# The hand-over from an expert's output to the next attention: an earlier second score, and small gate products among the long ones

## The chip, the cores and the metric

The kernel runs on one core of a Trainium2 chip. The metric is the device time of one execution in microseconds (us). TensorE multiplies matrices, ScalarE (ACT) and VectorE (DVE) read its results in PSUM, GpSimd (POOL) adds in SBUF, and SyncE (SP) mostly issues transfers.

## The reference

Eight sequences of 384 tokens go through grouped attention (16 heads of q, 4 of k and v, head size 64), and each token's attention output then goes to one of 16 experts, chosen by two softmaxes.

```python
def _attn_ref(q, k, v):
    ...                                      # k and v repeated for their group of 4 heads
    scores = scale * np.matmul(q, k.transpose(0, 1, 3, 2))
    scores = scores - np.max(scores, axis=-1, keepdims=True)
    attn = np.exp(scores)
    attn = attn / (np.sum(attn, axis=-1, keepdims=True) + 1e-09)
    return np.matmul(attn, v)

def _moe_ref(x, w_group, w_expert, w1, w2):  # x: 3072 tokens x 1024
    g_logits = x @ w_group                   # 4 groups
    g_idx = np.argmax(g_logits, axis=1)      # g_w: softmax weight of the chosen group
    for g in range(G):
        ...
        e_logits = xg @ w_expert[g]          # 4 experts a group; e_w likewise
        e_idx = np.argmax(e_logits, axis=1)
        for e in range(Eg):
            ...
            h = np.maximum(xg[mask_e] @ w1[g, e], 0.0)
            ye = h @ w2[g, e]
            out[tok_idx] = combined[:, None] * ye     # combined = g_w * e_w
```

## The kernel before

One sequence is one block `b` of work. The attention of `b` runs in 24 units (4 heads of k and v, 6 slices each). TensorE writes a score, ScalarE takes its exponential into SBUF, and TensorE multiplies that with v two units later.

```python
def score(self, u):
    ...
    sT = ps_tile("s")                        # two such tiles, in turn
    for r in range(2):
        for s in range(2):
            nc.tensor.matmul(out=sT[r * H2:(r + 1) * H2, s, :S], lhsT=kT..., rhs=qT...)   # 64x64
    e = epool.tile([P, 2, S], F32, name="e")
    nc.scalar.activation(e..., sT..., ACT.Exp, scale=scale)                               # line 311
...
def run(self, u0, u1, inserts, nxt=None):
    for u in range(u0, u1):
        if u + 2 < NU:
            self.score(u + 2)                # line 305
        ...
        self.pv(u)                           # line 324: 8 products of e with v
        self.tail(u)                         # adds on GpSimd, reductions on VectorE
        for f in inserts.get(u, []):
            f()
```

Before attention `b` is done, the expert of sequence `b` is not known. The kernel guesses it from the mean of v, works with that expert for the whole sequence, and tokens of other experts are done in a loop at the end. The guess needs 12 products with one column each (the means) and 4 products with 20 columns (the logits of the guess).

```python
def guess_mean(b, pt, eng=None):
    pm = pt[:, 1, :Hkv]
    v16 = vraw[b].rearrange("p h x -> p (h x)").bitcast(BF16)
    for g in range(Hkv):
        for i in range(SC):
            e0 = g * NC * D + i * P
            nc.tensor.matmul(out=pm[:, g:g + 1], lhsT=v16[:, 2 * e0 + 1:2 * (e0 + P):2],  # line 457
                             rhs=onesb[:, :1], start=(i == 0), stop=(i == SC - 1))
    vm = gpool.tile([P, Hkv], BF16, name="vm")
    evac(eng or nc.vector, vm, pm)
    return vm

def guess_logits(vm, glp):
    for g in range(Hkv):
        nc.tensor.matmul(out=glp[:, SC, :], lhsT=vm[:, g:g + 1].to_broadcast([P, P]),     # line 473
                         rhs=wgd[:, g, :], start=(g == 0), stop=(g == Hkv - 1))
```

Between two attentions the expert of the sequence before (`f = b - 1`) is worked off. Its output has three chunks `c` of 128 tokens; each chunk has two halves `nh` of 512 columns, and each half is a sum over 8 products.

```python
def ffn_y(w2, hT, c, which, nhs=(0, 1), y=None):
    if y is None:
        y = ps_tile(which)
    for nh in nhs:
        for f in range(FQ):                  # FQ = 8; line 615
            nc.tensor.matmul(out=y[:, nh, :], lhsT=hT[:, f, c * P:(c + 1) * P],
                             rhs=w2[:, f, nh * HALF:(nh + 1) * HALF],
                             start=(f == 0), stop=(f == FQ - 1))
    return y

def y_out(f, c, y, split=False):
    ...                                      # ScalarE and VectorE copy y times weight; then out
    if split:
        nc.scalar.mul(ot[:, :HALF], y[:, 0, :], weff[b][:, c:c + 1])                      # line 630
        nc.vector.tensor_scalar(ot[:, HALF:], y[:, 1, :], ...)                            # line 631

def block(b):
    last = b == B - 1
    f = b - 1
    ...                                      # transfers, first layer of f (L606), sums, normalise
    moe_y(f, 0, "s")
    cast(b, 2)
    cast(b, 3)
    nc.sync.dma_start(out=xb_dram[b], in_=xb[b])
    y = ffn_y(w2s[f], hTs[f], 1, "s", (0,))
    gate_logits(b, ps_tile("o"))             # line 443: 16 products
    ffn_y(w2s[f], hTs[f], 1, "s", (1,), y)
    y_out(f, 1, y)
    pt = ps_tile("s")
    glp = gate_rows(pt)
    gate_tokens(b, glp)                      # line 468: token logits, 3 products
    vm = None if last else guess_mean(b + 1, pt)
    y = ffn_y(w2s[f], hTs[f], 2, "o", (0,))
    if not last:
        guess_logits(vm, glp)
        at[b + 1] = Attn(b + 1)
        at[b + 1].score(0)
    weights[b] = gate_softmax(b, glp, not last)      # VectorE
    if not last:
        pick_index(b + 1)                            # VectorE
    ffn_y(w2s[f], hTs[f], 2, "o", (1,), y)
    if not last:
        at[b + 1].score(1)
        return {1: [do(y_out, f, 2, y, True)]}       # inserted behind unit 1 of the next attention
    ...
```

`block(b)` is called for b = 2 to 7. The hand-over from block 1 to attention 2 (`first_block`) is built alike, but does its gate work elsewhere.

Of the kernel before, what the change touches and what calls it, by code (L numbers as in the profile page):

```python
# [18 lines left out]
def kernel(  # L19
# [11 lines left out]
    nc = tc.nc  # L31
    P = 128
    B, Hq, S, D = q.shape
    _, Hkv, _, _ = k.shape
    SC = S // P
# [6 lines left out]
    FQ = F // P  # L42
    NW = G + NE
    HALF = DM // 2
# [26 lines left out]
    def ps_tile(which, shape=None, dtype=F32):  # L71
        if which == "x":
            which = f"o{1 - turn['o']}"
        else:
            turn[which] = 1 - turn[which]
            which += str(turn[which])
        return psum.tile(shape or [P, 2, 512], dtype, name="ps_" + which)
# [70 lines left out]
    onesb = cpool.tile([P, 4 * P], BF16)  # L148
# [38 lines left out]
    wgd = cpool.tile([P, Hkv, NW], BF16)  # L187
# [50 lines left out]
    def evac(eng, out_, in_):  # L238
        if eng is nc.scalar:
            eng.copy(out=out_, in_=in_)  # L240
        else:
            eng.tensor_copy(out=out_, in_=in_)  # L242
# [187 lines left out]
    def cast(b, m):  # L430
        ks = slice(2 * m, 2 * m + 2)
        nc.scalar.copy(out=xb[b][:, ks, :], in_=xT[b][:, ks, :])  # L432

    lgs = {}

    def gate_logits(b, pt):
        lg = pt[:, 0]
        for jj in range(KQ // 4):  # L440
            for t in range(4):
                kq = 4 * jj + t
                nc.tensor.matmul(out=lg[32 * t:32 * t + 32, :S], lhsT=wg[:, kq, :],  # L443
                                 rhs=xT[b][:, kq, :],
                                 start=(jj == 0), stop=(jj == KQ // 4 - 1))
        ls = gpool.tile([P, S], F32, name="lgs")
        nc.scalar.copy(out=ls, in_=lg[:, :S])
        lgs[b] = ls

    def guess_mean(b, pt, eng=None):  # L450

        pm = pt[:, 1, :Hkv]
        v16 = vraw[b].rearrange("p h x -> p (h x)").bitcast(BF16)
        for g in range(Hkv):
            for i in range(SC):
                e0 = g * NC * D + i * P
                nc.tensor.matmul(out=pm[:, g:g + 1], lhsT=v16[:, 2 * e0 + 1:2 * (e0 + P):2],  # L457
                                 rhs=onesb[:, :1], start=(i == 0), stop=(i == SC - 1))
        vm = gpool.tile([P, Hkv], BF16, name="vm")
        evac(eng or nc.vector, vm, pm)  # L460
        return vm

    def gate_rows(pt):
        return pt[:, 1, 64:64 + (SC + 1) * NW].rearrange("p (c n) -> p c n", n=NW)

    def gate_tokens(b, glp):
        for c in range(SC):
            nc.tensor.matmul(out=glp[:, c, :], lhsT=lgs[b][:, c * P:(c + 1) * P],  # L468
                             rhs=mod32[:, 0, :NW], start=True, stop=True)

    def guess_logits(vm, glp):
        for g in range(Hkv):
            nc.tensor.matmul(out=glp[:, SC, :], lhsT=vm[:, g:g + 1].to_broadcast([P, P]),
                             rhs=wgd[:, g, :], start=(g == 0), stop=(g == Hkv - 1))

    def gate_softmax(b, glp, guess, eng=None):

# [75 lines left out]
    ers, w1s, w2s = {}, {}, {}  # L553
# [3 lines left out]
    def pick_index(b):  # L557
        oh = oh_first if b == 0 else oh_all[:, b - 1, SC, :]
        key = gpool.tile([P, NE], F32, name="key")
        nc.vector.scalar_tensor_tensor(key, oh, float(NE), eback, op0=ALU.mult, op1=ALU.add)  # L560
        km = gpool.tile([P, 1], F32, name="km")
        nc.vector.tensor_reduce(out=km, in_=key, axis=AX.X, op=ALU.max)
        oh1 = oh1_all[:, b, :]
        nc.vector.tensor_scalar(oh1, key, km, None, op0=ALU.is_ge)
        t1 = gpool.tile([P, NE], F32, name="t1")
        ef = gpool.tile([P, 1], F32, name="ef")
        nc.vector.scalar_tensor_tensor(t1, eidx, 1.0, oh1, op0=ALU.mult, op1=ALU.mult,
                                       accum_out=ef)
        e_i = gpool.tile([P, 1], I32, name="e_i")
        nc.vector.tensor_copy(out=e_i, in_=ef)  # L570
        e_is[b] = e_i
# [35 lines left out]
                                 rhs=x[:, kq, :], start=(kq == 0), stop=(kq == KQ - 1))  # L607
        nc.scalar.activation(hT[:, f0:f0 + 2, :], h[:, :, :S], ACT.Relu)  # L608

    def ffn_y(w2, hT, c, which, nhs=(0, 1), y=None):  # L610
        if y is None:
            y = ps_tile(which)
        for nh in nhs:
            for f in range(FQ):
                nc.tensor.matmul(out=y[:, nh, :], lhsT=hT[:, f, c * P:(c + 1) * P],  # L615
                                 rhs=w2[:, f, nh * HALF:(nh + 1) * HALF],
                                 start=(f == 0), stop=(f == FQ - 1))
        return y

    hTs = {}  # L620

    def moe_h(b, f0, which):
        if f0 == 0:
            hTs[b] = xpool.tile([P, FQ, S], BF16, name="hT", bufs=1)
        ffn_h(xb[b], w1s[b], hTs[b], f0, which)
# [15 lines left out]
    def do(f, *a):  # L641
        return lambda: f(*a)
# [6 lines left out]
    at = {0: Attn(0), 1: Attn(1)}  # L649
    at[0].start()  # L650
    fill(4)
    state, weights = {}, {}
# [11 lines left out]

    def first_guess():
        state["pt"] = ps_tile("x")
        state["vm"] = guess_mean(0, state["pt"], nc.scalar)

    def first_pick():
        glp = gate_rows(state["pt"])  # L670
        guess_logits(state["vm"], glp)
        first_choice(glp)
        pick_index(0)

# [19 lines left out]
    a = at[0]  # L694
# [19 lines left out]
    a = at[1]  # L714
# [10 lines left out]
    pt = ps_tile("x")  # L725
    gate_logits(0, pt)
    moe_h(0, 2, "s")
    glp = gate_rows(pt)
    gate_tokens(0, glp)
    vm = guess_mean(1, pt, nc.scalar)  # L730
    collect(1, 0, 2)
    sums(1, 0, 2, "s")
    for m in range(2):
        normalise(1, m)
    moe_h(0, 4, "s")
    guess_logits(vm, glp)
    weights[0] = gate_softmax(0, glp, True, nc.scalar)
    pick_index(1)
    moe_h(0, 6, "s")
# [3 lines left out]
    def first_block():  # L743

        prefetch(1)
        collect(1, 2, Hkv)
        weights[0]()
        out_weights(0)
        cast(1, 0)
        cast(1, 1)  # L750
        moe_y(0, 0, "s")
        y = ffn_y(w2s[0], hTs[0], 1, "s", (0,))
        sums(1, 2, Hkv, "o")
        normalise(1, 2)
        normalise(1, 3)
        ffn_y(w2s[0], hTs[0], 1, "s", (1,), y)
        y_out(0, 1, y)
        cast(1, 2)
        cast(1, 3)
        nc.sync.dma_start(out=xb_dram[1], in_=xb[1])  # L760
        y = ffn_y(w2s[0], hTs[0], 2, "o", (0,))
        at[2] = Attn(2)
        at[2].score(0)
        ffn_y(w2s[0], hTs[0], 2, "o", (1,), y)
        at[2].score(1)
        return {1: [do(y_out, 0, 2, y, True)], 3: [second_logits], 19: [second_gate],
                21: [second_pick]}

# [3 lines left out]
    def second_gate():  # L772
        state["pt"] = ps_tile("x")
        gate_tokens(1, gate_rows(state["pt"]))
        state["vm"] = guess_mean(2, state["pt"])

    def second_pick():
        glp = gate_rows(state["pt"])
        guess_logits(state["vm"], glp)
        weights[1] = gate_softmax(1, glp, True, nc.scalar)  # L780
        pick_index(2)

# [9 lines left out]
# [3 lines that stand above are left out]
        prefetch(b)  # L795
        moe_h(f, 0, "s")
        collect(b, 0, Hkv)
        weights[f]()
        out_weights(f)
        moe_h(f, 2, "s")  # L800
        sums(b, 0, Hkv, "o")
        for m in range(4):
            normalise(b, m)
        moe_h(f, 4, "s")
        moe_h(f, 6, "s")
        cast(b, 0)
        cast(b, 1)
        moe_y(f, 0, "s")
        cast(b, 2)
        cast(b, 3)  # L810
        nc.sync.dma_start(out=xb_dram[b], in_=xb[b])
        y = ffn_y(w2s[f], hTs[f], 1, "s", (0,))
        gate_logits(b, ps_tile("o"))
        ffn_y(w2s[f], hTs[f], 1, "s", (1,), y)
        y_out(f, 1, y)
        pt = ps_tile("s")
        glp = gate_rows(pt)
        gate_tokens(b, glp)
        vm = None if last else guess_mean(b + 1, pt)
        y = ffn_y(w2s[f], hTs[f], 2, "o", (0,))  # L820
        if not last:
            guess_logits(vm, glp)
            at[b + 1] = Attn(b + 1)
            at[b + 1].score(0)
        weights[b] = gate_softmax(b, glp, not last)
        if not last:
            pick_index(b + 1)
        ffn_y(w2s[f], hTs[f], 2, "o", (1,), y)
        if not last:
            at[b + 1].score(1)  # L830
            return {1: [do(y_out, f, 2, y, True)]}
        y_out(f, 2, y, True)
        weights[b]()
        out_weights(b)
# [26 lines left out]
    for c in range(SC):  # L861
        ot = opool.tile([P, DM], F32, name="ot")
        for nh in range(2):
            y = ps_tile("so"[nh])
# [12 lines left out]
            for i, (ps, x) in enumerate(halves(c)):  # L877
                eng = nc.scalar if (c, nh, i) == (SC - 1, 1, 1) else nc.sync
# [5 lines left out]
    with tc.For_i(0, n_left, 1):  # L884
# [17 lines left out]
        w1, w2 = fetch1(er), fetch2(er)  # L902
# [8 lines left out]
        hT = xpool.tile([P, FQ, S], BF16, name="hT", bufs=1)  # L911
# [4 lines left out]
        for c in range(SC):  # L916
# [3 lines left out]
            y = ffn_y(w2, hT, c, "s")  # L920
# [34 lines left out]
```

The softmax here doesn't subtract the row's maximum and nothing guards it: scores larger than these inputs give would overflow.

## Time and profile before

| | |
|---|---|
| device time, median of 3 runs | 382.23 us (382.09 to 382.82) |
| span of the profiled execution | 380.1 us |
| matmuls on TensorE | 3663 |
| granted TensorE clock, mean | 0.996 |
| VectorE / ScalarE / GpSimd busy | 69% / 61% / 39% of the span |
| moved by DMA | 76.02 MB, 200 GB/s in the mean |

The profile is that of one execution. Its lines name the engine, the line of the kernel, the output and the inputs of a group of instructions, and the shapes. PE is TensorE's multiplying part, PEld its loading of weights, which can overlap. The chain that ended last follows the work back from the last instruction to what released each step, so a step on it is one that the end of the kernel hung on, and "issue" is time in which the engine waited for nothing that the profile shows. The end of a matmul is modelled, while starts are recorded; distances are therefore best taken from start to start.

### The profile page before, as it was taken

The numbers are of one execution on the slowest core, as the hardware profiler recorded it, in microseconds if no ns is written. First come the engines' busy times: TensorE is split into PE (matmuls) and PEld (weight loads), VectorE is DVE, ScalarE is ACT, GpSimd is POOL, SyncE is SP. The second block draws the span as 40 slices with busy tenths as digits, with TensorE's granted clock in tenths as the row PEclk, the third lists the DMA queues.
The fourth block names the chain that finished last, engine by engine and source line by source line (L and its number), as shares of the span: only waits on it lengthen the run. The fifth ranks groups of instructions, "written<-read, shape, count | busy, mean of one in ns | idle before, by whom it ended". The sixth has DMA issues, their size and how long they took to land.

```text
span 380.1 us, 8950 instructions
## 1 busy us (share of the span) xinstructions
PE 364.6 (96%) x3663; PEld 193.9 (51%) x3663; DVE 261.9 (69%) x494; ACT 232.6 (61%) x315; POOL 147.3 (39%) x116
## 2 busy tenths in 40 slices
PE   8999799999989999999999999999999999999992
PEld 3444356444545455545555455554555456554541
DVE  4789978847689279854998279883798449983130
ACT  4779945768824498256953489344982569544321
POOL 5657730716613077212653047330772036600000
PEclk9999999999999999999999999999999999999998
DMA  8975999999999999899999999999998999199734
GB/s 190 247 115 93 238 211 149 241 237 260 207 160 223 252 248 184 173 211 297 213 148 221 228 278 208 148 220 254 244 185 163 182 282 228 30 207 220 236 68 100
DMA packets 71209, 76.02 MB, mean 200 GB/s; under 512 B 35928, under 2 KB 50264, under 8 KB 71168
## 3 DMA queue, kind: packets, MB, share of 16 engines
q0 software_dynamic: 26640, 41.03, 61.8%
q1 hardware_dynamic: 44096, 33.81, 36.1%
q10 hardware_dynamic: 432, 0.61, 0.5%
q8 instruction: 29, 0.48, 0.5%
q14 instruction: 12, 0.10, 0.1%
HBM read 89.21 MB, written 18.87 MB: 284 GB/s over the span
## 4 chain that ended last, share of the span: by engine, by line
PE 78%; DVE 13%; ACT 6%; issue 2%; ACTq 0%; DVEq 0%; POOLq 0%
PE ps_o L324 22%; PE ps_s L606 18%; PE ps_s L615 14%; PE ps_o L615 7%; PE ps_s L305 7%; ACT e L311 4%; DVE red L338 4%; PE ps_o L443 3%; DVE xT L425 2%; DVE rb L416 2%; PE ps_o L268 1%; PE ps_o L606 1%; DVE w L425 1%; PE ps_s L468 1%; PE ps_o L405 1%
## 5 line engine op out<-in xcount | busy, mean ns | idle before, releaser
L331 POOL TENSOR_TENSOR e<-e 128x768 f32<-128x768 f32 x64 | 116.1, 1830 | 138.5 <-ACT e L311 91.5
L311 ACT ACTIVATE e<-ps_s 128x768 f32<-128x768 f32 x192 | 149.1, 819 | 25.2 <-PE ps_s L305 23.5
L324 PE MATMUL ps_o<-e,v_raw 64*64 64x384 f32 x1536 | 153.8, 482 | 1.6 <-DVE xT L425 1.6
L338 DVE TRANSPOSE_TENSOR_REDUCE red<-e 128x24 f32<-128x768 f32 x128 | 114.1, 946 | 10.5 <-POOL e L331 10.5
L606 PE MATMUL ps_s<-xb,w 128*128 128x384 bf16 x480 | 81.0, 326 | 0.0
L324 PEld LDWEIGHTS ps_o<-e,v_raw 64*64 64x64 f32 x1536 | 61.0, 133 | 28.5 <-issue 20.0
L305 PE MATMUL ps_s<-qT,kT 64*64 64x384 bf16 x768 | 67.1, 327 | 3.0 <-ACT e L311 1.7
L608 ACT ACTIVATE hT<-ps_s 128x768 bf16<-128x768 f32 x30 | 24.3, 811 | 70.9 <-PE ps_s L606 70.9
L606 PEld LDWEIGHTS <-w 128*128 128x128 bf16 x512 | 48.8, 98 | 36.3 <-issue 4.8
L615 PEld LDWEIGHTS <-hT 128*128 128x128 bf16 x384 | 36.0, 98 | 45.4 <-issue 5.4
L615 PE MATMUL ps_s<-w,hT 128*128 128x512 bf16 x248 | 56.4, 379 | 0.0
L305 PEld LDWEIGHTS <-kT 64*64 64x64 bf16 x768 | 29.4, 104 | 42.6 <-issue 39.1
L615 PE MATMUL ps_o<-w,hT 128*128 128x512 bf16 x136 | 32.0, 379 | 0.0
L416 DVE STREAM_TRANSPOSE rb<-inv 128x384 f32<-128x384 f32 x60 | 31.1, 557 | 1.0
L425 DVE TENSOR_TENSOR xT<-xT,rb 128x768 f32<-128x768 f32 x26 | 28.2, 1086 | 0.9
L634 ACT ACTIVATE ot<-ps_s,we 128x1024 f32<-128x1024 f32 x14 | 15.6, 1116 | 19.1 <-PE ps_s L615 19.1
L432 ACT CAST xb<-xT 128x768 bf16<-128x768 f32 x28 | 22.1, 832 | 0.0
L371 DVE COPY xT<-ps_o 128x768 f32<-128x768 f32 x22 | 20.2, 919 | 0.0
L242 DVE CAST vm<-ps_s 128x4 bf16<-128x4 f32 x5 | 0.8, 163 | 27.4 <-PE ps_s L457 27.4
L663 POOL COPY after<-qT 128x1 bf16<-128x1 bf16 x7 | 1.3, 189 | 40.5 <-DMA qT<-q_raw 37.5
L631 DVE TENSOR_SCALAR ot<-ps_o,we 128x512 f32<-128x512 f32 x7 | 5.3, 750 | 15.6 <-ACT ot L630 11.3
L409 DVE RECIPROCAL inv<-ps_o 128x96 f32<-128x96 f32 (+2 forms) x10 | 6.0, 603 | 7.0 <-PE ps_o L405 7.0
(129 smaller groups left out, 189.3 us busy)
## 6 DMA issues: line engine op xcount, KB each, us to landing
w<-in_moe_w_dram POOLq DMA_DIRECT2D x16, 2048.0 KB, 21.9
out_dram<-ot SPq DMA_DIRECT2D x42, 256.0 KB, 7.0
xb_scratch<-xb SPq DMA_DIRECT2D x8, 768.0 KB, 9.8
q_raw<-in_q_dram POOLq DMA_DIRECT2D x7, 768.0 KB, 33.6
v_raw<-in_v_dram SPq DMA_DIRECT2D x14, 384.0 KB, 7.3
out_dram<-ot SPq DMA_DIRECT2D x11, 128.0 KB, 2.3
k<-in_k_dram POOLq DMA_DIRECT2D x7, 192.0 KB, 30.3
w<-in_q_dram POOLq DMA_DIRECT2D x3, 192.0 KB, 7.3
```

The lines of the kernel that those rows point to most:

```text
L305: nc.tensor.matmul(out=sT[r * H2:(r + 1) * H2, s, :S], lhsT=kT[b][s * D:(s + 1) * D, slot, ks], rhs=qT[b][s * D:(s + 1) * D, kq * SC:(kq + ...
L311: nc.scalar.activation(e.rearrange("p t (s x) -> p s t x", s=2), sT[:, :, :S].rearrange("p s (t x) -> p s t x", t=2), ACT.Exp, scale=scale)
L324: nc.tensor.matmul(out=oT[t * D:(t + 1) * D, r, :S], lhsT=vraw[b][r * H2:(r + 1) * H2, g, c * D:(c + 1) * D], rhs=self.e[u][r * H2:(r + 1) ...
L331: eng.tensor_add(out=self.e[u], in0=self.e[u], in1=self.e[u + 1])
L338: nc.vector.tensor_reduce(out=reds[self.b][:, g, n].rearrange("p t j -> p (t j)"), in_=self.e[u].rearrange("p t (j x) -> p (t j) x", x=32) ...
L371: nc.vector.tensor_copy(out=dst, in_=src)
L416: nc.vector.transpose(out=rb[:, r].rearrange("p (j x) -> p j x", x=32), in_=inv[b][:, 2 * m + r].unsqueeze(2).to_broadcast([P, NB, 32]))
L425: eng.tensor_mul(out=x, in0=x, in1=rb)
L432: nc.scalar.copy(out=xb[b][:, ks, :], in_=xT[b][:, ks, :])
L606: nc.tensor.matmul(out=h[:, jj, :S], lhsT=w1[:, kq, (f0 + jj) * P:(f0 + jj + 1) * P], rhs=x[:, kq, :], start=(kq == 0), stop=(kq == KQ - 1))
L608: nc.scalar.activation(hT[:, f0:f0 + 2, :], h[:, :, :S], ACT.Relu)
L615: nc.tensor.matmul(out=y[:, nh, :], lhsT=hT[:, f, c * P:(c + 1) * P], rhs=w2[:, f, nh * HALF:(nh + 1) * HALF], start=(f == 0), stop=(f == ...
```

## The change

The second score of the next attention came behind the whole second half of the expert's last chunk. It now comes after three of the eight products of that half, so that ScalarE can begin its exponential while TensorE still has five products to do. `first_block` gets this too. And in blocks 2 to 6 the 12 mean products and the 4 guess products no longer stand in rows of their own: a helper, `weave`, puts them between the products of the middle chunk, the means into its first half and the guess into its second. The means move into the free bank of the tile of the gate logits, the softmax of the gate and the choice of the expert are issued before the first score, and no product is added or left out.

```diff
+    def weave(main, side):
+        k = 0
+        for i, f in enumerate(main):
+            f()
+            while k < len(side) and k * len(main) < (i + 1) * len(side):
+                side[k]()
+                k += 1
 ...
-    def ffn_y(w2, hT, c, which, nhs=(0, 1), y=None):
+    def ffn_y(w2, hT, c, which, nhs=(0, 1), y=None, fs=None, side=()):
         if y is None:
             y = ps_tile(which)
-        for nh in nhs:
-            for f in range(FQ):
-                nc.tensor.matmul(...)
+        weave([mm(...) for nh in nhs for f in (range(FQ) if fs is None else fs)], side)
         return y
+
+    def y_scores(f, a, y):
+        ffn_y(w2s[f], hTs[f], 2, "o", (1,), y, range(FQ // 2 - 1))
+        a.score(1)
+        ffn_y(w2s[f], hTs[f], 2, "o", (1,), y, range(FQ // 2 - 1, FQ))
 ...  # first_block
-        ffn_y(w2s[0], hTs[0], 2, "o", (1,), y)
-        at[2].score(1)
+        y_scores(0, at[2], y)
 ...  # block
-        y = ffn_y(w2s[f], hTs[f], 1, "s", (0,))
-        gate_logits(b, ps_tile("o"))
-        ffn_y(w2s[f], hTs[f], 1, "s", (1,), y)
+        gt = ps_tile("o")
+        y = ffn_y(w2s[f], hTs[f], 1, "s", (0,), side=[] if last else guess_mean(b + 1, gt))
+        gate_logits(b, gt)
+        glp = gate_rows(ps_tile("s"))
+        guess = [] if last else guess_logits(mean_copy(gt, nc.vector), glp)
+        ffn_y(w2s[f], hTs[f], 1, "s", (1,), y, side=guess)
         y_out(f, 1, y)
-        pt = ps_tile("s")
-        glp = gate_rows(pt)
         gate_tokens(b, glp)
-        vm = None if last else guess_mean(b + 1, pt)
         y = ffn_y(w2s[f], hTs[f], 2, "o", (0,))
-        if not last:
-            guess_logits(vm, glp)
-            at[b + 1] = Attn(b + 1)
-            at[b + 1].score(0)
         weights[b] = gate_softmax(b, glp, not last)
         if not last:
             pick_index(b + 1)
+            at[b + 1] = Attn(b + 1)
+            at[b + 1].score(0)
+            y_scores(f, at[b + 1], y)
+            return {1: [do(y_out, f, 2, y, True)]}
         ffn_y(w2s[f], hTs[f], 2, "o", (1,), y)
-        if not last:
-            at[b + 1].score(1)
-            return {1: [do(y_out, f, 2, y, True)]}
```

More of the change, by code (lines that the diff above doesn't have):

```diff
@@ L432, in cast, with mm @@
         nc.scalar.copy(out=xb[b][:, ks, :], in_=xT[b][:, ks, :])
+    def weave(main, side):
[5 more added lines that the diff above has]
+                k += 1
+    def mm(*a, **kw):
+        return lambda: nc.tensor.matmul(*a, **kw)
     lgs = {}
@@ L448, in gate_logits, with guess_mean @@
         lgs[b] = ls
-    def guess_mean(b, pt, eng=None):
+    def guess_mean(b, pt):
         pm = pt[:, 1, :Hkv]
         v16 = vraw[b].rearrange("p h x -> p (h x)").bitcast(BF16)
+        side = []
         for g in range(Hkv):
@@ L456, in guess_mean, with mean_copy, all_of @@
                 e0 = g * NC * D + i * P
-                nc.tensor.matmul(out=pm[:, g:g + 1], lhsT=v16[:, 2 * e0 + 1:2 * (e0 + P):2],
-                                 rhs=onesb[:, :1], start=(i == 0), stop=(i == SC - 1))
+                side.append(mm(out=pm[:, g:g + 1], lhsT=v16[:, 2 * e0 + 1:2 * (e0 + P):2],
+                               rhs=onesb[:, :1], start=(i == 0), stop=(i == SC - 1)))
+        return side
+    def mean_copy(pt, eng):
         vm = gpool.tile([P, Hkv], BF16, name="vm")
-        evac(eng or nc.vector, vm, pm)
+        evac(eng, vm, pt[:, 1, :Hkv])
         return vm
+    def all_of(side):
+        for f in side:
+            f()
     def gate_rows(pt):
@@ L471, in guess_logits @@
     def guess_logits(vm, glp):
-        for g in range(Hkv):
-            nc.tensor.matmul(out=glp[:, SC, :], lhsT=vm[:, g:g + 1].to_broadcast([P, P]),
-                             rhs=wgd[:, g, :], start=(g == 0), stop=(g == Hkv - 1))
+        return [mm(out=glp[:, SC, :], lhsT=vm[:, g:g + 1].to_broadcast([P, P]), rhs=wgd[:, g, :],
+                   start=(g == 0), stop=(g == Hkv - 1)) for g in range(Hkv)]
     def gate_softmax(b, glp, guess, eng=None):
@@ L608, in ffn_h @@
         nc.scalar.activation(hT[:, f0:f0 + 2, :], h[:, :, :S], ACT.Relu)
-    def ffn_y(w2, hT, c, which, nhs=(0, 1), y=None):
+    def ffn_y(w2, hT, c, which, nhs=(0, 1), y=None, fs=None, side=()):
         if y is None:
             y = ps_tile(which)
-        for nh in nhs:
-            for f in range(FQ):
-                nc.tensor.matmul(out=y[:, nh, :], lhsT=hT[:, f, c * P:(c + 1) * P],
-                                 rhs=w2[:, f, nh * HALF:(nh + 1) * HALF],
-                                 start=(f == 0), stop=(f == FQ - 1))
-        return y
+        weave([mm(out=y[:, nh, :], lhsT=hT[:, f, c * P:(c + 1) * P],
+                  rhs=w2[:, f, nh * HALF:(nh + 1) * HALF], start=(f == 0), stop=(f == FQ - 1))
+               for nh in nhs for f in (range(FQ) if fs is None else fs)], side)
+        return y
+    def y_scores(f, a, y):
+        ffn_y(w2s[f], hTs[f], 2, "o", (1,), y, range(FQ // 2 - 1))
+        a.score(1)
+        ffn_y(w2s[f], hTs[f], 2, "o", (1,), y, range(FQ // 2 - 1, FQ))
     hTs = {}
@@ L666, in first_guess @@
         state["pt"] = ps_tile("x")
-        state["vm"] = guess_mean(0, state["pt"], nc.scalar)
+        all_of(guess_mean(0, state["pt"]))
+        state["vm"] = mean_copy(state["pt"], nc.scalar)
     def first_pick():
         glp = gate_rows(state["pt"])
-        guess_logits(state["vm"], glp)
+        all_of(guess_logits(state["vm"], glp))
         first_choice(glp)
@@ L729 @@
     gate_tokens(0, glp)
-    vm = guess_mean(1, pt, nc.scalar)
+    all_of(guess_mean(1, pt))
+    vm = mean_copy(pt, nc.scalar)
     collect(1, 0, 2)
@@ L735 @@
     moe_h(0, 4, "s")
-    guess_logits(vm, glp)
+    all_of(guess_logits(vm, glp))
     weights[0] = gate_softmax(0, glp, True, nc.scalar)
@@ L774, in second_gate @@
         gate_tokens(1, gate_rows(state["pt"]))
-        state["vm"] = guess_mean(2, state["pt"])
+        all_of(guess_mean(2, state["pt"]))
+        state["vm"] = mean_copy(state["pt"], nc.vector)
     def second_pick():
         glp = gate_rows(state["pt"])
-        guess_logits(state["vm"], glp)
+        all_of(guess_logits(state["vm"], glp))
         weights[1] = gate_softmax(1, glp, True, nc.scalar)
@@ L811, in block @@
         nc.sync.dma_start(out=xb_dram[b], in_=xb[b])
-        y = ffn_y(w2s[f], hTs[f], 1, "s", (0,))
-        gate_logits(b, ps_tile("o"))
-        ffn_y(w2s[f], hTs[f], 1, "s", (1,), y)
+        gt = ps_tile("o")
[4 more added lines that the diff above has]
+        ffn_y(w2s[f], hTs[f], 1, "s", (1,), y, side=guess)
         y_out(f, 1, y)
-        pt = ps_tile("s")
-        glp = gate_rows(pt)
         gate_tokens(b, glp)
-        vm = None if last else guess_mean(b + 1, pt)
         y = ffn_y(w2s[f], hTs[f], 2, "o", (0,))
-        if not last:
-            guess_logits(vm, glp)
-            at[b + 1] = Attn(b + 1)
-            at[b + 1].score(0)
         weights[b] = gate_softmax(b, glp, not last)
```

## The prediction

> **What bounds the kernel now.** I read the busy shares first. TensorE is busy for nearly all of the span, and its clock is granted in full (the row of granted clock is nines until the end), so time is lost or won on TensorE's own queue.
>
> ```profile
> PE 364.6 (96%) x3663; PEld 193.9 (51%) x3663; DVE 261.9 (69%) x494; ACT 232.6 (61%) x315; POOL 147.3 (39%) x116
> ```
>
> Next I read the chain that ended last, cut to the place the change touches: the end of the expert's output in the middle of the run and the first units of the attention behind it (columns: start in us, length in us, what).
>
> ```profile
> 168.21 1.43 PE ps_o L443 x16
> 169.63 1.83 PE ps_s L615 x8
> 171.47 0.58 PE ps_s L468 x6
> 172.04 0.28 PE ps_s L457 x12
> 172.33 1.75 PE ps_o L615 x8
> 174.08 0.09 PE ps_s L473 x4
> 174.16 0.29 PE ps_s L305 x4
> 174.45 1.83 PE ps_o L615 x8
> 176.28 0.32 PE ps_s L305 x4
> ...
> 178.08 0.82 ACT e L311
> 178.90 0.58 ACT ot L630
> 179.47 0.71 ACT e L311
> 180.18 0.04 issue
> 180.22 0.36 PE ps_s L305 x4
> 180.58 0.64 PE ps_o L324 x8
> 181.23 0.16 PE ps_s L305 x4
> ```
>
> L443 are gate logits, L468 token logits, L457 the 12 products of the means of v, L473 the four guess products, L615 half a chunk of expert output (8 products), L305 a score, L324 a unit of attention times v. The reader is to see three things. The 12 means take 0.28 us, 23 ns each; the guess products 0.09 us. A score inside the attention takes 0.16 us, but one between two expert halves 0.29, and the half behind it 1.83 instead of 1.75. And from 176.6 to 180.2 the chain runs through ScalarE: the exponentials, with the copy of the expert's output (L630) between two of them.
>
> Windows of a fraction of a microsecond in the timeline give the starts that I calculate with. For TensorE:
>
> ```profile
> 174.09 0.36 PE L305 MATMUL ps_s<-qT,kT 64*64 64x384 bf16 x4
> 174.38 0.39 PE L615 MATMUL ps_o<-w,hT 128*128 128x512 bf16 x1
> ...
> 176.21 0.52 PE L305 MATMUL ps_s<-qT,kT 64*64 64x384 bf16 x8
> ```
>
> and for ScalarE, in windows of its own:
>
> ```profile
> 176.68 0.81 ACT L311 ACTIVATE e<-ps_s 128x768 f32<-128x768 f32 x1 [1.31 <-PE ps_s L305]
> ...
> 178.77 0.70 ACT L630 ACTIVATE ot<-ps_o,we 128x512 f32<-128x512 f32 x1
> 179.34 0.83 ACT L311 ACTIVATE e<-ps_s 128x768 f32<-128x768 f32 x1
> ```
>
> The stretch repeats every 44.2 us: L606's second half starts at 157.72, 201.92, 246.12 and 290.31 in the chain.
>
> **What the Trainium skill says.** "TensorE: Matmul & The Clock Gate", section "Wait — 56ns, not 53.3ns?", has the distance between starts of small matmuls never below about 25 ns, however small they are; the trace's 0.28/12 = 23 ns agrees, and here each also brings its own weights. The same page, section "Step-by-step: what each phase is for", has weight loads pulled ahead of running matmuls into a background buffer; agreed, the 98 ns loads of L615 lie hidden under products that follow each other every 216 ns. "TensorEngine Tiling (Array Packing)", section "Key Properties", says that a change of tiling mode drains TensorE. Agreed: a score (64x64) between expert products (128x128) costs more than one in the stream. "PSUM — Partial Sum Buffer", section "PSUM bank collisions raise a hardware error", asks for guards by bank. The means go to one bank of the tile and gate logits to the other, so VectorE may copy the means while gate logits run; no run shows this yet.
>
> **Part 1, the weave.** It removes no product. It moves 12 means from behind the token logits between the first eight products of chunk 1, and 4 guess products between its second eight. Could weight loads now vanish under the long products? A mean's load does. But the next long product's load can then start only once the mean has taken its own weights, so the exposed load moves from the mean to the product behind it. The trace shows that price: the last mean starts at 171.89 + 11 x 0.025 = 172.17, the product behind it at 172.19, 0.02 to 0.03 us later. So 12 x 0.025 = 0.30 us leave one place and 0.30 us come in at the other. For the guess products I take 4 x 0.025 = 0.10 us against 0.09: 0.01 to 0.02 us lost. The softmax chain of the gate can start some 2 us earlier on VectorE, which waits for L473 there; nobody on the path waits for its result. Sum: 0, at worst -0.02 us in each of the five blocks.
>
> **Part 2, the second score.** Count from the start of the first score. Rules from the trace: score to next product 0.29 (174.09 to 174.38); eight product starts take to 175.90, so first to second 0.23, then 0.216 each; last product to score 0.31 (175.90 to 176.21); score after a mode change 0.19, in the stream 0.16; unit of L324 0.645, thus 0.81 a unit; score start to exponential start 0.47 (174.09 to 174.56; 176.21 to 176.68); exponential to exponential 0.70 (2.22 us for three, the last 0.81); to the output copy 0.69; from there to the next exponential 0.57; start of an exponential to the score that needs its buffer 0.88 (179.34 to 180.22).
>
> Before: score 6 starts at 180.22 - 174.09 = 6.13. Without waits it would be 0.29 + 1.52 + 0.31 (score 1 at 2.12) + 0.35 (two scores) + 0.645 + 3 x 0.81 = 5.54, so 0.59 us are waits: score 3 on exponential 1 (0.33), score 6 on exponential 4 behind the copy (0.26).
>
> After: three products at 0.29, 0.52, 0.73; score 1 at 1.04; five at 1.33 to 2.21; score 2 at 2.52; L324 at 2.71; scores 3, 4, 5 at 3.35, 4.16, 4.97; score 6 at 5.78 if nothing waits. The extra trip from 128x128 to 64x64 and back costs 5.78 - 5.54 = 0.24 us. ScalarE: exponential 0 at 0.47, 1 at 1.51 (score 3's buffer free at 2.39: its wait is gone), 2 at 2.99, 3 at 3.82 (its score decides), the copy at 4.51, exponential 4 at 5.08. Score 6 needs that one: 5.08 + 0.88 = 5.96, a wait of 0.18. Later ones fit (score 7 needs exponential 5, at 5.78 + 0.88 = 6.66, and comes at 6.77). Gain: 6.13 - 5.96 = 0.17 us. The 0.59 us of waits are thus mostly spent on the trip and on the wait that remains.
>
> This holds for the five middle blocks. In the first block the chain differs:
>
> ```profile
> 81.21 0.83 ACT xb L432
> 82.04 0.72 ACT e L311
> 82.76 0.04 issue
> 82.80 0.36 PE ps_s L305 x4
> ```
>
> Exponential 0 stands behind a cast that waits for VectorE, and score 2 waits for it at 82.80. An earlier score 1 does not free it: score 2 could come at 80.03 + 2.52 = 82.55 and still waits to 82.80. Gain there 0. The last block has no next attention, so gain 0.
>
> **Sum.** 5 x (0.17 - 0.02) = 0.75 us: 382.23 - 0.75 = 381.5; I say 381.4, since the small terms behind the copy may be a little kinder.
>
> **Rivals.** (a) The copy on ScalarE does not stand in the way, say because score 6 is a little later than I count. Then 0.18 more each, 0.9 us in all: 380.5. For it: it is a matter of 0.2 us. Against: the order of ScalarE's queue is unchanged. (b) Woven products are free, because their whole cost hides in the gaps of the long ones: 5 x 0.37 = 1.9 us, with part 2 then 379.6. For it: TensorE loads weights in the background, and that must be the author's idea. Against: the start of the product behind the last mean, 0.02 to 0.03 us later and with a load of its own. (c) Weaving spoils the look-ahead, and a whole 98 ns load shows at each woven product: 16 x 0.075 x 5 = 6 us, 387.5. Against: the same start. (d) Transfers take over. DMA is near full in most slices (nines in that row), and the loads are chained: GpSimd sits 37.5 us in all in wait for transposed q before it can ask for weights. But a block's q lands near 203 and its first score is at 218, and weights are asked for at 204, take some 22 us, and are used at 240. Over ten microseconds of slack swallow five gains of 0.2: if this were wrong, 382.2. (e) VectorE's copy of the means comes too late for the first guess product. It has the gate logits' 1.43 us for a copy of 0.16; if the two banks were guarded as one, the copy would wait for the gate logits and cost 0.2 us a block, 382.4.
>
> **Range and chances.** (a) and half of (b) give the low end, 380.0; (e) or a woven price of some 35 ns instead of 25 gives the high end: 16 x 0.01 x 5 = 0.8, 382.2, and with what runs differ (382.09 to 382.82) 382.8. Two per cent are 7.6 us: above, only (c) comes near; below, even (a) with (b) gives 2.7 us or so, 0.7%. So within 2% at 0.96.
>
> **What would show it.** In the chain of the changed kernel: no L457 and L473 of their own, but the halves with L615 grown to 1.73 + 0.30 and 1.83 + 0.10; a score between three and five products, with some 0.29 around it; no wait at score 3; a wait of 0.1 to 0.2 at score 6 behind L630; block period 44.05 instead of 44.2. Halves that stay at 1.75 would prove (b), halves of 2.5 or more (c); a period that stays, with new waits on DMA, (d).

## The result, and the profile after

The changed kernel takes 385.11 us (384.88 to 385.45), the kernel before 382.47 in the same comparison. The ratio is 1.007, with a 95% interval of 1.0052 to 1.0087. That is slower by 2.0 to 3.3 us, within 2% as forecast, but outside the predicted range and on the other side of the kernel before.

The block period shows where it comes from. I take it from the second halves of the first layer in the chain that ended last. The kernel before (start, length, what; the first line is the first expert product):

```profile
49.93 2.71 PE ps_s L606 x16
...
157.72 5.31 PE ps_s L606 x32
...
334.51 5.30 PE ps_s L606 x32
```

The same places after the change:

```profile
50.55 2.71 PE ps_s L625 x16
...
158.93 5.30 PE ps_s L625 x32
...
337.48 5.31 PE ps_s L625 x32
```

(334.51 - 157.72) / 4 = 44.20 us before and (337.48 - 158.93) / 4 = 44.64 us after, so a block has grown by 0.44. From the first line to the last it is 284.58 us before and 286.93 after, 2.35 more. The remaining 0.3 of the 2.64 between the medians is not traced to the change: the start of the first expert product, ahead of everything that was edited, varies by some 1.1 us over the profiles of this study.

The next view is the chain of the changed kernel, at the stretch that the prediction showed of the kernel before. L446 is now the line of all products that go through the helper (long ones, means and guess); L455 are the gate logits, L488 the token logits, L459 ScalarE's copy of the gate logits.

```profile
169.69 1.47 PE ps_o L455 x16
171.16 0.02 issue
171.19 0.49 ACT lgs L459
171.67 0.02 issue
171.70 0.17 DVE vm L242
171.87 0.05 issue
171.91 1.78 PE ps_s L446 x11
173.70 0.58 PE ps_s L488 x6
174.28 1.73 PE ps_o L446 x8
176.01 0.29 PE ps_s L305 x4
176.30 0.75 PE ps_o L446 x3
177.05 0.29 PE ps_s L305 x4
177.34 1.18 PE ps_o L446 x5
178.52 0.29 PE ps_s L305 x4
178.81 0.65 PE ps_o L324 x8
...
181.88 0.35 PE ps_s L305 x4
```

Two things have changed places. In this attention the chain no longer leaves TensorE for ScalarE's exponentials. Ahead of it, between the gate logits and the second half of the middle chunk, it now does leave TensorE: for ScalarE's copy of the gate logits, then for VectorE's copy of the means. The timeline there, all engines:

```profile
171.05 0.39 PE L446 MATMUL ps_s<-w,hT 128*128 128x512 bf16 x1
171.19 0.48 ACT L459 COPY lgs<-ps_o 128x384 f32<-128x384 f32 x1 [0.90 <-PE ps_o L455]
171.70 0.16 DVE L242 CAST vm<-ps_o 128x4 bf16<-128x4 f32 x1 [3.70 <-ACT lgs L459]
171.91 0.10 PEld L446 LDWEIGHTS <-vm 128*128 128x128 bf16 x1 [0.77 <-DVE vm L242]
171.91 0.18 PE L446 MATMUL ps_s<-wgd,vm 128*128 128x20 bf16 x1 [0.47 <-DVE vm L242]
```

One long product runs at 171.05. The guess product behind it could start 0.216 us later, at 171.27, and starts at 171.91: 0.64 us lost, the same within 0.01 in all five blocks. The last mean starts at 169.53, but VectorE, idle for 3.70 us, copies them only at 171.70, and what it waited for is not the means and not even the gate logits, but ScalarE's copy of the gate logits. That copy reads the other bank of the same tile (a PSUM tile here has two halves of 512 columns, `[:, 0]` and `[:, 1]`, one bank each) and has nothing to do with the means.

### The profile page after: what moved, and what is told of

The parts are those of the page before. It is cut to its first block, busy times and chain, and to the rows that moved or that the text cites. A ratio compares the mean times of both kernels' runs of the same rounds, so it can differ in the third digit from the quotient of the medians.

```text
span 383.4 us, 8950 instructions
## 1 busy us (share of the span) xinstructions
PE 366.3 (96%) x3663; PEld 192.0 (50%) x3663; DVE 261.8 (68%) x494; ACT 233.6 (61%) x315; POOL 147.1 (38%) x116
## 4 chain that ended last, share of the span: by engine, by line
PE 81%; DVE 13%; ACT 3%; issue 1%; DVEq 0%; ACTq 0%; POOLq 0%
PE ps_o L324 25%; PE ps_s L625 18%; PE ps_s L446 14%; PE ps_s L305 8%; PE ps_o L446 7%; DVE red L338 4%; PE ps_o L455 3%; DVE xT L425 2%; ACT e L311 2%; DVE rb L416 2%; PE ps_o L268 2%; PE ps_o L625 1%; DVE w L425 1%; PE ps_s L488 1%; PE ps_o L405 1%
## 5 line engine op out<-in xcount | busy, mean ns | idle before, releaser
L446 PE MATMUL ps_s<-w,hT 128*128 128x512 bf16 x248 | 58.9, 379 | 0.0
L446 PEld LDWEIGHTS <-hT 128*128 128x128 bf16 x384 | 35.2, 99 | 40.9 <-issue 6.4
L305 PEld LDWEIGHTS <-kT 64*64 64x64 bf16 x768 | 28.6, 104 | 43.8 <-issue 40.1
L446 PE MATMUL ps_o<-w,hT 128*128 128x512 bf16 x136 | 33.0, 380 | 0.0
L242 DVE CAST vm<-ps_o 128x4 bf16<-128x4 f32 x6 | 1.0, 162 | 19.2 <-ACT lgs L459 18.0
L242 DVE COPY gl<-ps_s 128x80 f32<-128x80 f32 (+1 forms) x6 | 1.4, 239 | 17.6 <-PE ps_s L488 17.6
```

The lines of the kernel that those rows point to most:

```text
L446: return lambda: nc.tensor.matmul(*a, **kw)
```

## The experiments

Three theories stood against each other. W: all of the loss is this one wait. S: the earlier second score costs more than it gives. P: small products are dearer between long ones than in rows. "Period" is always the block period as above, and "score 6" is counted from the start of score 0 of the same attention, in attentions 4 to 7. Kernels of one comparison share the runs of the kernel before.

| kernel | ratio (95%) | period, us | score 6, us |
|---|---|---|---|
| before | 1 | 44.20 | 6.13 |
| changed | 1.007 (1.0052 to 1.0087) | 44.64 | 5.93 |
| second score alone | 0.9979 (0.9972 to 0.9987) | 44.00 | 5.93 |
| weave alone | 1.0083 (1.0066 to 1.0100) | 44.84 | 6.13 |
| changed, means in a tile of their own | 0.9980 (0.9970 to 0.9989) | 43.99 | 5.93 |
| changed, copy of the means ahead of ScalarE's copy | 0.9988 (0.9979 to 0.9997) | 44.13 | 5.93 |
| changed, copy of the means ahead of the gate logits | one run, no interval | 44.32 | 5.93 |
| own tile, early output copy | 0.9943 (0.9924 to 0.9961) | 43.80 | 5.77 |
| own tile, both scores first, early output copy | 0.9915 (0.9898 to 0.9932) | 43.57 | 5.54 |
| own tile, both scores first, late output copy | 0.9957 (0.9939 to 0.9974) | 43.76 | 5.70 |

### The second score alone

The small products stay in rows as they were before.

```diff
-        ffn_y(w2s[f], hTs[f], 2, "o", (1,), y)
-        if not last:
-            at[b + 1].score(1)
+        if not last:
+            y_scores(f, at[b + 1], y)        # 3 products, score 1, 5 products; in first_block too
```

> The earlier second score alone, the small gate products left in rows as in the kernel before. Theory W (the whole loss is one wait: VectorE's copy of the means waits for ScalarE's copy of the gate logits out of the same tile, and the first woven guess product waits 0.65 us for it in each of five blocks): block period 44.0 us against 44.20, score 6 about 5.95 us behind score 0, time 1.0 us below the kernel before, ratio 0.997 to 0.998. Theory S (the earlier score costs more than it gives): period above 44.2, ratio above 1.000. Theory P (the small products are dearer between long ones): the same as W here.

Measured: ratio 0.9979, 0.83 us off the 382.66 of the kernel before, period 44.00, score 6 at 5.93. Theory S falls: the earlier score is a gain, of 0.20 us in each of attentions 4 to 7. In attention 3, the first that the five blocks hand over to, score 6 comes at 6.10 and gains only 0.03: there exponential 2 starts 0.75 us behind its score instead of 0.47, after a pause of ScalarE in which the profile shows no wait (in the changed kernel the same, at 6.11). Why it pauses there is open; in three of the kernels further below score 6 comes in attention 3 as early as in the others. So the sum, 0.83, is near the 5 x 0.17 = 0.85 of the prediction partly by luck.

### The weave alone

```diff
-            y_scores(f, at[b + 1], y)
+            ffn_y(w2s[f], hTs[f], 2, "o", (1,), y)
+            at[b + 1].score(1)
```

> The weave alone, the second score behind the whole half as before. W: period 44.20 + 0.65 = 44.8 us, time 3.1 to 3.3 us above the kernel before, ratio 1.0085, and one wait of 0.65 us ahead of the first guess product. S: no loss here, ratio 1.000. P: ratio above 1.007, but spread over the 16 products, with starts 0.05 us or more behind one another instead of 0.025.

Measured: ratio 1.0083, thus 3.2 us (the medians, of 4 and 39 runs, are 2.6 apart), period 44.84, thus 0.64 a block. The tile of the means answers the same way as in the changed kernel: VectorE sat idle for 18.0 us in five waits until ScalarE's copy of the gate logits was done. The two parts add up: 44.00 + 44.84 - 44.20 = 44.64, the period of the changed kernel.

### The means in a tile of their own

Weave and score stay as changed, and only the place of the means moves: to the other ps_o tile, which is free until the last chunk.

```diff
         gt = ps_tile("o")
-        y = ffn_y(..., side=[] if last else guess_mean(b + 1, gt))
+        mt = None if last else ps_tile("x")
+        y = ffn_y(..., side=[] if last else guess_mean(b + 1, mt))
 ...
-        guess = [] if last else guess_logits(mean_copy(gt, nc.vector), glp)
+        guess = [] if last else guess_logits(mean_copy(mt, nc.vector), glp)
```

> The changed kernel, but the means go to a tile of their own (the other ps_o tile) and not to the second bank of the gate logits' tile. W: the copy of the means waits for the means alone, the wait of 0.65 us is gone, period 44.0 us, time about 1.0 us below the kernel before, ratio 0.997 to 0.998. P: the products still stand between long ones, so the loss stays: period 44.6, ratio 1.007. S: the loss stays too.

Measured: ratio 0.9980, period 43.99. The same stretch of the chain in this kernel (start, length, what):

```profile
169.32 1.43 PE ps_o L455 x16
170.75 1.93 PE ps_s L446 x12
172.68 0.58 PE ps_s L488 x6
```

And from its timeline the last mean and the copy of the means:

```profile
169.15 0.16 PE L446 MATMUL ps_o<-onesb,v_raw 128*128 128x1 bf16 x1
169.36 0.16 DVE L242 CAST vm<-ps_o 128x4 bf16<-128x4 f32 x1 [1.74 <-PE ps_o L446]
```

The copy runs 0.21 us behind the last mean, beside the gate logits, though it is still issued behind ScalarE's copy of them. So it was not the order of issue that held it in the changed kernel, but the shared tile. TensorE is not left between the gate logits and the next half. That half holds 8 long and 4 guess products and takes 1.93 us, 0.10 more than the 1.83 of the kernel before: the 4 x 0.025 of the prediction. Theory P falls. And against the second score alone (44.00), the whole weave without its wait is worth 0.01 us a block, which is nothing.

### The two copies exchanged

Is it only the two readers of a tile that are put in a row? Same tiles as in the changed kernel, but VectorE's copy is issued ahead of ScalarE's.

```diff
-    def gate_logits(b, pt):
+    def gate_logits(b, pt, between=None):
         ...                                  # 16 products
+        vm = between() if between else None  # mean_copy(pt, nc.vector)
         nc.scalar.copy(out=ls, in_=lg[:, :S])
```

> The changed kernel, same tiles, but VectorE's copy of the means is issued ahead of ScalarE's copy of the gate logits (behind the gate logits' products). W, if only the two readers of one tile are put in a row: the copy runs as soon as the means are there, beside the gate logits, nothing waits, period 44.0, ratio 0.998. W, if the whole tile is guarded against its writer too: the copy waits for the last gate logit, the first guess product waits some 0.2 us, period 44.2, ratio 1.000. P and S: 44.6, ratio 1.007.

Measured: ratio 0.9988, period 44.13, between the two cases but with the wait of the second. Its timeline, all engines:

```profile
171.02 0.39 PE L446 MATMUL ps_s<-w,hT 128*128 128x512 bf16 x1
171.15 0.16 DVE L242 CAST vm<-ps_o 128x4 bf16<-128x4 f32 x1 [3.19 <-PE ps_o L455]
171.35 0.48 ACT L460 COPY lgs<-ps_o 128x384 f32<-128x384 f32 x1 [1.09 <-DVE vm L242]
171.37 0.10 PEld L446 LDWEIGHTS <-vm 128*128 128x128 bf16 x1 [0.26 <-DVE vm L242]
```

VectorE waits for the last gate logit (L455), which writes the other bank, and ScalarE now waits for VectorE. So both banks of the tile are guarded as one: whoever uses one bank waits for the users of the other, a reader for a writer as well as a reader for a reader. The guess product starts at 171.37 instead of 171.02 + 0.216 = 171.24: 0.13 us, which is the 0.14 between 44.13 and 43.99.

### The copy ahead of the gate logits' products

```diff
+        vm = None if last else mean_copy(gt, nc.vector)
         gate_logits(b, gt)
         glp = gate_rows(ps_tile("s"))
-        guess = [] if last else guess_logits(mean_copy(gt, nc.vector), glp)
+        guess = [] if last else guess_logits(vm, glp)
```

> The changed kernel, same tiles, but VectorE's copy of the means is issued ahead of the gate logits' products. If the whole tile is guarded, both banks as one (as the 0.14 us left in the run with the two copies exchanged suggest): the gate logits now wait for that copy, some 0.4 us behind the last mean, no wait at the first guess product, period 44.3. If only banks are guarded: no wait at either place, period 44.0.

Measured (one run): period 44.32. The wait now stands ahead of the gate logits, in the timeline of this kernel:

```profile
168.79 0.16 PE L446 MATMUL ps_o<-onesb,v_raw 128*128 128x1 bf16 x1
169.00 0.16 DVE L242 CAST vm<-ps_o 128x4 bf16<-128x4 f32 x1 [1.74 <-PE ps_o L446]
169.21 0.16 PEld L455 LDWEIGHTS ps_o<-xT,wg 128*32 128x32 f32 x8 [0.54 <-DVE vm L242]
169.22 0.85 PE L455 MATMUL ps_o<-xT,wg 128*32 128x384 f32 x8 [0.26 <-DVE vm L242]
```

The last mean is at 168.79, the gate logits at 169.22, 0.43 us later; in the changed kernel that distance was 0.09 (169.53 to 169.62). 0.34 us are lost there, as the period says: 44.32 - 43.99 = 0.33. Wherever the copy stands, sharing the tile costs something: 0.64 behind ScalarE's copy, 0.14 behind the gate logits, 0.33 ahead of them.

### Better than both: the output copy early, and one trip instead of two

The prediction left two costs standing in the attention's start: a wait of 0.18 at score 6 behind the output copy, and 0.24 for the second trip between tiling modes. Three kernels take them away, all with the means in their own tile. In the first, ScalarE's half of the output copy is issued behind the second half's products instead of inside the attention:

```diff
             y_scores(f, at[b + 1], y)
-            return {1: [do(y_out, f, 2, y, True)]}
+            y_first(f, 2, y)                 # ScalarE's half of y_out
+            return {1: [do(y_rest, f, 2, y)]}    # VectorE's half, and out
```

> Means in a tile of their own, and ScalarE's half of the output copy issued right behind the second score's half, ahead of exponential 2, instead of between exponentials 3 and 4. If that copy is what score 6 still waits for: score 6 at 5.78 us behind score 0 instead of 5.93, period 43.84 instead of 43.99, ratio to the kernel before 0.996. If score 6 waits for something else: 43.99 and 0.998.

Measured: ratio 0.9943, period 43.80, score 6 at 5.77. So it was the copy.

In the second, score 1 also comes right behind score 0, ahead of all eight products (blocks 2 to 6):

```diff
-            y_scores(f, at[b + 1], y)
+            at[b + 1].score(1)
+            ffn_y(w2s[f], hTs[f], 2, "o", (1,), y)
```

> As the run with the early output copy, but in blocks 2 to 6 score 1 stands right behind score 0, ahead of the last eight products, so that there is one trip between tiling modes and not two. If the trip costs the 0.24 us that the prediction reckoned: score 6 at 5.57 us, nothing waits for exponentials, period 43.63, ratio 0.9925. If score 1 has to wait for its tile or the trip is cheap: 43.8 or more, ratio 0.995 or more.

Measured: ratio 0.9915, 378.86 us against 382.80, period 43.57, score 6 at 5.54. Its chain stays on TensorE through the whole hand-over:

```profile
172.10 1.73 PE ps_o L446 x8
173.84 0.45 PE ps_s L305 x8
174.28 1.83 PE ps_o L446 x8
176.12 0.29 PE ps_s L305 x4
176.40 0.65 PE ps_o L324 x8
177.05 0.16 PE ps_s L305 x4
```

Two scores together take 0.45 us, 0.16 more than one. ScalarE's timeline in this kernel also has a further sign of the guard by tile:

```profile
174.23 1.51 ACT L311 ACTIVATE e<-ps_s 128x768 f32<-128x768 f32 x2 [1.56 <-PE ps_s L305]
176.16 0.69 ACT L665 ACTIVATE ot<-ps_o,we 128x512 f32<-128x512 f32 x1 [0.41 <-PE ps_o L446]
176.74 4.62 ACT L311 ACTIVATE e<-ps_s 128x768 f32<-128x768 f32 x6
```

L665 is the output copy; it reads the first half of the chunk, finished before the scores, and yet waits for the products of the second half in the other bank. Here that costs nothing.

The third has both scores first, but the output copy in its old place:

> As the run with both scores first, but the output copy in its old place between exponentials 3 and 4. If the copy and the trip add up: score 6 waits 0.19 us for exponential 4, at 5.76, period 43.82, ratio 0.9955. If the copy no longer matters once both scores are early: 43.63, ratio 0.9925.

Measured: ratio 0.9957, period 43.76, score 6 at 5.70, a wait of 0.16. The copy and the trip add up, and each is worth what its step said.

## Why the prediction was wrong

**The step that failed is the overlap in part 1: VectorE was to copy the means while the gate logits run, so that no guess product waits.** It waits 0.64 us in each of five blocks. The prediction had the mechanism before it, as rival (e), and put it aside: "It has the gate logits' 1.43 us for a copy of 0.16; if the two banks were guarded as one, the copy would wait for the gate logits and cost 0.2 us a block, 382.4." Neither half of that sentence held. The copy did not get the gate logits' time, because a tile of two banks is guarded as one here; the two kernels that move the copy, and the one that moves the means, show it. And the price was set too low: a copy that waits only for the gate logits costs 0.14 (the exchanged copies), but it was issued behind ScalarE's copy out of the same tile, and so the 0.48 us of that copy and 0.02 to 0.03 from its end to the next start came on top: 0.64. Five times 0.64 are 3.2 us. 44.20 - 0.20 + 0.64 = 44.64 closes the account of a block.

What led to the error was how the skill was used. "PSUM — Partial Sum Buffer", section "PSUM bank collisions raise a hardware error", says by which unit accesses must be kept apart: bank and quadrant, by bank in the simple form. The prediction took that for the unit in which this program's waits are set. They are set by tile. A hint stood in the profile before and was not weighed: VectorE's half of the output copy waited for ScalarE's half in six cases, though the two read different banks of one tile. The group's line on the page of the kernel before (busy, mean of one, then idle time ahead of it and what ended most of it):

```profile
L631 DVE TENSOR_SCALAR ot<-ps_o,we 128x512 f32<-128x512 f32 x7 | 5.3, 750 | 15.6 <-ACT ot L630 11.3
```

This line alone does not settle it, since the two halves also write one tile of SBUF; it was a reason to ask.

**Part 1, the weave, was right in its own cost.** The changed kernel's timeline shows the means between the long products:

```profile
168.25 0.19 PE L446 MATMUL ps_o<-onesb,v_raw 128*128 128x1 bf16 x2
168.30 0.38 PE L446 MATMUL ps_s<-w,hT 128*128 128x512 bf16 x1
168.51 0.16 PE L446 MATMUL ps_o<-onesb,v_raw 128*128 128x1 bf16 x1
168.54 0.38 PE L446 MATMUL ps_s<-w,hT 128*128 128x512 bf16 x1
```

From 168.30 to 168.54 are 0.24 us with one mean in between, against 0.216 without: 0.025 a mean, the price that it had in its row (the prediction's 23 ns are the length of the row in the chain divided by 12; the starts lie 0.025 apart). What was saved behind the token logits came back between the long products, so rivals (b) and (c) are both out. That this price is the weight load of the product behind the mean is the prediction's reading; no run tests it.

**Part 2 was right to some hundredths in four of its five attentions.** Score 6 at 5.96 was predicted, 5.93 measured (6.11 in attention 3, where nearly nothing was gained); the wait at score 3 is gone, a wait of 0.16 at score 6 is left, and the early output copy shows that it is the one named. In the first block the gain was to be 0: from score 0 to the gate logits behind unit 3 the distance is 6.24 us before and after. Of rival (a) therefore nothing came without moving the copy, and moved it brought 0.19. Transfers, rival (d), did not take over even at a period of 43.57.

So a block was predicted at -0.15 and came at +0.44; the difference of 0.59 is the one wait of 0.64, less 0.05 by which the rest was kinder than reckoned. Over the whole kernel 5 x 0.64, less 4 x 0.20 and the 0.02 of attention 3, are 2.38 us; the profiles show 2.35. What stays open is the pause of ScalarE in attention 3, and the 0.3 us to the 2.64 of the medians, which lie inside the interval.

## What to carry to other kernels

Before a product moves earlier, follow its result to the consumer, and read from the program which events that consumer really waits for; a second user of the same tile can put itself in between, even when it touches another bank. Small products that already followed one another every 0.025 us gained nothing here from standing between long ones. When a handful of scores is pulled ahead of other work, try them together, one change of tiling mode for all (0.23 us a block here), and look next at what else ScalarE has to do before it can free their buffers.

## What the runs showed that was not expected

In this program the two banks of one tile in PSUM act as one for waits between engines: reader behind reader (0.64 us at the guess product), reader behind writer (0.14) and writer behind reader (0.33). A tile of its own for the means, of which they use 16 bytes a partition, removed all three. The weave itself, 16 products moved in each of five blocks, changed the period by 0.01 us.
